# A chain of attention, MLP and routed experts on one core: the early table from six chunks of nine, for four groups

## The chip, the core and the metric

The kernel runs on one core of a Trainium2 chip. The metric is the device time of one execution in microseconds (us). Three runs of the kernel before have a median of 1148.74 us (1147.65 to 1150.2). The traced execution, from which every duration below comes, took 1151.18 us by the same clock; its span from the first to the last instruction is 1149.2 us.

## The reference, cut to what matters

```python
attn_out = _attn_ref(q, k, v)          # 4 batches, 8 heads, 576 positions, window 128
x = attn_out as 2304 tokens x 512
h = x @ w_in                           # 512 -> 2048
x = softplus(h) @ w_out                # 2048 -> 512: the tokens of the routed part
noisy = x @ w_gate + softplus(x @ w_noise) * noise
top2, top2_w = two best of 8 experts of each token, softmax over the two
for e in range(8):                     # each token goes through two experts
    out[its tokens] += weight * (relu(x[its tokens] @ w1[e]) @ w2[e])
```

## The kernel before, in words

The 2304 tokens are worked in nine **chunks** of 256 (numbers 0 to 8). The first MLP has 16 weight tiles of each of its two matrices. All chunks run its first six tiles, with the attention of the next chunk fed in between; then, one chunk after another, the other ten. A **job** is one tile of one chunk: 12 matmuls into `h`, the softplus on ACT, DVE and POOL (`mm1`, lines 564 to 574), and three jobs later 6 matmuls into `y` (`mm2`).

After its last job a chunk is routed in small steps between the jobs that follow (`route`): transposes, logits, the two best experts, and in `r_rank` each token's place in its expert's list. Four indirect DMAs per chunk from POOL (line 771) scatter the token numbers and weights into four copies of the lists in DRAM (`rect`). `mcum` holds the count of each expert so far.

The experts work on **groups**: a pair of 128 tokens of one expert (256 together), or a single 128 at the end of a list. `early_table` and `late_table` compute on DVE, in one partition, which expert and which place in its list each group has. The early table takes experts that already have 256 tokens when some chunks are still missing; the late table takes the rest. For each group `g_rows` (lines 1025 to 1039) reads the place into a register of SP, issues four small loads of the lists (`rk`, line 1032) on SP's queue, and chains a `merge` of the four copies (two short DVE reductions into `rc`, lines 1036 and 1037). `g_gather` then fetches the 256 tokens with two indirect DMAs on POOL (`xg`, line 1047); PE transposes them (`t<-ident,xg`) while the group ahead is computed, and ACT and DVE split them into `xh` and `xl` (lines 1065 and 1066).

A group has eight weight tiles of 512 KB, loaded by SP at line 1111 once the group's table is done (`raw2`, named raw in the rows, for four of them, else `rawp` in the ring of 24 slots that the first MLP's weights also use). `w2_split` makes `whi` on ACT (line 1140) and `wlo` on DVE (line 1138) from each. A pair of groups' outputs is scaled into `ys` and added into `out` by two indirect DMAs on POOL per group (line 1252); each waits for the DMA of the one before it.

Nothing is scheduled at run time. A planner (`Order`) keeps a clock of its own while the program is written out; a `chain` puts each step on its engine's queue when the planner thinks its turn has come, and the queues then run in that order. Two facts of it matter here. The SP work of `g_rows` costs nothing on the planner's clock, and a `merge` is queued a fixed time, `after=6.0`, after its loads are issued, whatever they take. A weight tile's `whi` is queued when the planner's clock has run 512 KB at 280 GB/s and 2 us more.

The main loop counts jobs with `t`. `last_start` is the first job of chunk 8's second part. `open_p2` (which frees the attention's memory and opens the pool of the tables) runs at `last_start`, and `early_table(NCH - 3)`, the table of chunks 0 to 6, one job later.

Of the kernel before, what the change touches and what calls it, by code (L numbers as in the profile page):

```python
# [25 lines left out]
class Order:  # L26
# [11 lines left out]
    def chain(self, *steps, after=0.0):  # L38

        heapq.heappush(self.heap, (self.now + after, self.count, steps, 0))  # L40
        self.count += 1
# [28 lines left out]
    def emitted(self, key):  # L70
        while key not in self.fin:
            assert self.heap, key
            self._pop()

    def need(self, key):
        self.emitted(key)
        self.now = max(self.now, self.fin[key])
# [35 lines left out]
def moe_chain_kernel(ctx, tc, qk, v, w_in, w_out, w_gate, w_noise, noise, w1, w2, out):  # L113
# [3 lines left out]
    T = B * S  # L117
    DM = H * D
    KC = DM // P
    NF = w_in.shape[0]  # L120
    E, NW1 = w1.shape[:2]
    NF1 = 2 * NW1
    CT = 256
    TT = CT // P
    NCH = T // CT
# [5 lines left out]
    NA = 6  # L131
    NCV = 5
    NPAIR = (2 * T // P + E - 1) // 2 - 3
    NSING = E - 1
    NEARLY = 5
    NOPT = 2
    NLATE = NPAIR - NEARLY
    TPAD = T + P
# [5 lines left out]
    chain, spend, need, emitted, mark = o_.chain, o_.spend, o_.need, o_.emitted, o_.mark  # L144
# [13 lines left out]
    def f32(ap):  # L158
        return ap.bitcast(F32)
# [3 lines left out]
    def tl(pool, shape, dtype, name, bufs, fin, tag=None, slots=None):  # L163

        r = rings.setdefault(name, [])
        while len(r) >= bufs:
            last = r[-bufs]
            (need if pool is psum else emitted)(last)
            if r[-bufs] == last:
                break  # L170
        r.append(fin)
        return pool.tile(shape, dtype, name=name, tag=tag or name, bufs=slots or bufs)
# [3 lines left out]
    def few_t():  # L176

        for k_ in rings["t"][-4:]:
            emitted(k_)
        nt[0] = 2  # L180
# [64 lines left out]
    x1buf = dram.tile([TPAD, DM], F32, name="x1buf")  # L245
# [13 lines left out]
    def prepare1():  # L259
        n = NREC // P  # L260
        pad = mid.tile([P, n, 2], I32, name="pad", bufs=1)
        POOL.iota(pad[:, :, 0], pattern=[[1, n]], base=0, channel_multiplier=n)
        DVE.tensor_scalar(pad[:, :, 0], pad[:, :, 0], P - 1, T, op0=OP.bitwise_and, op1=OP.bitwise_or)
        POOL.memset(f32(pad[:, :, 1]), 0.0)
        for r in rect:
            SP.dma_start(r.rearrange("(p n) z -> p (n z)", p=P), pad.rearrange("p n z -> p (n z)"))
# [193 lines left out]
    def attn_until(c):  # L460
        return 4 * attn_last(c) + 3 + LC + 1
# [148 lines left out]
    def x_load(c):  # L610
        XT[c] = tuple(tl(mid, [P, KC, CT], F32R, n, 2, ("mm1b", c)) for n in ("xh", "xl"))
        for z, x in enumerate(XT[c]):
            dma(lambda z=z, x=x: SP.dma_start(f32(x).rearrange("p k t -> p (k t)"), xspill[c, z]),
                ("xi", c, z), 1 << 19)
# [221 lines left out]
    def row(name, shape, dtype=F32):  # L836
        return p2.tile([1] + shape, dtype, name="c_" + name, tag="c_" + name, bufs=1)

    def open_p2():
        nonlocal p2  # L840
        for m in range(NM):
            emitted(("c", m))
        astack.close()
        p2 = ctx.enter_context(tc.tile_pool(name="p2", bufs=2))
        few_t()
        for name, n, base, step in (("jm", NJ, 0, P), ("jpair", NJ // 2, P, 2 * P), ("jfull", NJ // 2, 2 * P, 2 * P),
                                    ("e8", E, 0, 1), ("qe", NEARLY, 0, 1), ("qp", NLATE, 0, 1), ("qs", NSING, 0, 1)):
            t = TB[name] = row(name, [n])
            POOL.iota(t, pattern=[[step, n]], base=base, channel_multiplier=0, allow_small_or_imprecise_dtypes=True)
# [76 lines left out]
    def counted(c, name):  # L926

        need(("mc", c))
        pc = ps_t(("pc", c))[:, :E]
        mm(pc, ones, mcum, True, True)  # L930
        tb = Table(name)
        cnt = tb.row("cnt", [E])
        tb.tensor_copy(cnt, pc[0:1, :])
        tb.steps[-1] += (("pc", c),)
        return tb, cnt

    def early_table(c):
        tb, cnt = counted(c, "E")
        per = tb.above("per", cnt, TB["jfull"], NJ // 2, OP.is_ge)
        inc = tb.upto("inc", per)  # L940
        ex, r = tb.first_of(TB["qe"], "q", NEARLY, inc, per)
        tb.finish("early", ex, r, None, NEARLY)
        a, b = tb.row("a", [E]), tb.row("b", [E])
        tb.tensor_sub(b, inc, per)
        tb.tensor_scalar(a, inc, float(NEARLY), None, op0=OP.min)
        tb.tensor_scalar(b, b, float(NEARLY), None, op0=OP.min)
        tb.tensor_sub(a, a, b)
        off = TB["off"] = tb.row("off", [E])
        tb.tensor_scalar(off, a, 2.0 * P, None, op0=OP.mult)
        chain(*tb.steps, (None, 0.0, early_lists, ("tab", 0), (("scat", c),)))  # L950
# [73 lines left out]
    def g_rows(g):  # L1024

        n, eo, i = groups[g]
        eo = TB[eo]
        r0 = SP.value_load(eo[0:1, 1, i:i + 1], min_val=0, max_val=E * T)
        rc = tl(p2, [P, 2, 2], I32, "rc", 6, ("gdone", g))
        rk = tl(p2, [P, NCOPY, 2, 2], I32, "rk", 6, ("rows", g))  # L1030
        for k in range(NCOPY):
            SP.dma_start(rk[:, k, :n, :], rect[k][bass.ds(r0, n * P), :].rearrange("(a p) z -> p a z", p=P))  # L1032

        def merge():

            DVE.tensor_reduce(rc[:, :n, 0], rk[:, :, :n, 0].rearrange("p k a -> p a k"), axis=AX.X, op=OP.min)
            DVE.tensor_reduce(f32(rc[:, :n, 1]), f32(rk[:, :, :n, 1]).rearrange("p k a -> p a k"), axis=AX.X, op=OP.add)
        chain(("V", 0.4, merge, ("rows", g)), after=6.0)
        GR[g] = dict(rc=rc)

    def g_gather(g):
        n, eo, i = groups[g]
        d = GR[g]
        d["xg"] = []
        for a in range(n):
            x = tl(p2, [P, DM], F32, "xg", 6, ("gx", g, a))
            POOL.indirect_dma_start(out=x, out_offset=None,
                                    in_=x1buf[:T - 2 * CT if g < NEARLY else TPAD, :],
                                    in_offset=bass.IndirectOffsetOnAxis(ap=d["rc"][:, a, 0:1], axis=0))
            d["xg"].append(x)  # L1050

# [233 lines left out]
    def pieces_of(c):  # L1285
        for s in range(attn_until(c), attn_until(c + 1)):
            yield from attn_step(s)
# [4 lines left out]
    last_start = NT - (NF - NA)  # L1292
# [38 lines left out]
    for t in range(NT + max(L2, len(items) + 2)):  # L1331
        if t == 4:
            SP.dma_start(wgn[:, :, :E], w_gate.rearrange("(c p) e -> p c e", p=P))
            SP.dma_start(wgn[:, :, E:2 * E], w_noise.rearrange("(c p) e -> p c e", p=P))
            SP.dma_start(nz, noise.rearrange("(a p) e -> p a e", p=P))
        if t == 20:
            prepare1()
        if t > 40 and t % 2:
            p = next(zfeed, None)
            if p is not None:  # L1340
                p()
        due[0] = min(NSL, 2 * NA + max(0, t - 2 * NA + 2) // 2)
        if t in starts:
            c, n = starts[t]
            if feed is not None:
                for p in feed:
                    p()
            feed = pieces_of(c) if c + 1 < NCH else None
            total = 2 * (attn_until(c + 1) - attn_until(c)) if feed else 0
            fed, gap, gaps = 0, 0, 2 * n - 2  # L1350
        if t == last_start:
            open_p2()
        if t == last_start + 1:
            early_table(NCH - 3)
        if t < NT:
            c, fc = jobs[t]
            if c == NCH - 1 and fc == 1:
                x_load(0)
            mm1(c * NF + fc)
            if c == 0 and fc == NA + 3:  # L1360
                part_load(0)
            used(2 * fc, c)
            if NT - 3 < t:
                if t == NT - 2:
                    need(("gl", 0))
                g_transpose(0, t - NT + 2)
                if t == NT - 1:
                    turned.add(0)
                    if 3 in REG:
                        g_start(3)  # L1370
        else:
            phase2(t - NT)
        side_work()
        if 0 <= t - L2 < NT:
            c, fc = jobs[t - L2]
            mm2(c * NF + fc)
            used(2 * fc + 1, c)
            if fc == NA - 1:
                part_evac(c)
            if fc == NF - 1:  # L1380
                y_evac(c)
                rfeed = chained(rfeed, route(c))
        if 0 <= t - NT - 2 < len(items):
            s3(*items[t - NT - 2])
        side_work()
# [64 lines left out]
```

## Time and profile before

| | |
|---|---|
| median of three runs | 1148.74 us |
| traced execution | 1151.18 us, span 1149.2 us |
| mean granted clock of TensorE | 0.973 |
| PE busy | 1075.3 us (94%) |
| DVE, ACT, POOL busy | 751.0, 616.7, 518.2 us (65%, 54%, 45%) |
| chain that ended last | PE 79%, DVE 10%, DMA 3%, ACT 3%, issue 2%, SP's queue 2%, POOL 1% |

In the span's picture in 40 slices PE has 8 tenths or more in every slice from the third on but the 22nd (about 603 to 632 us) and the last one: the 22nd is at 4, and the granted clock there is at 7. That is where the last chunk of the first MLP goes over into the experts.

### The profile page before, as it was taken

Reading aid. Unit: us, or ns where it says so; the run is one execution under the profiler, and the core shown is the slowest. Engines: PE = TensorE matmul, PEld = TensorE weight load, DVE = VectorE, ACT = ScalarE, POOL = GpSimd, SP = SyncE. Lnnn points to the kernel's source line nnn. Section 1 sums busy time; section 2 is a strip of 40 time slices with the busy share of each in tenths; the row PEclk is TensorE's granted clock in tenths of the full one; section 3 lists DMA queues with packets and bytes.
Section 4 is the critical chain, followed back from the end, with each engine's and each line's share of the span. In section 5 each row is a group of like instructions: output and inputs, shape, how many; then the busy total and the mean of one; then the engine's idle time right before and its main releaser. Section 6 shows DMA issues by size and latency. Waiting matters only on the chain.

```text
span 1149.2 us, 20936 instructions
## 1 busy us (share of the span) xinstructions
PE 1075.3 (94%) x7021; PEld 916.9 (80%) x7021; DVE 751.0 (65%) x1946; ACT 616.7 (54%) x1459; POOL 518.2 (45%) x535
## 2 busy tenths in 40 slices
PE   5589998999999999999994999999999999999997
PEld 3377776777789888888873889999799799799984
DVE  7975698999785677777764678665355355355520
ACT  7776678877664444444433445555455455455531
POOL 3455577776675566666654341323223223233212
PEclk8789999999999999999997999999999999999999
DMA  8231444564583322211217976988888888888722
GB/s 302 101 92 56 161 152 164 173 227 154 187 316 120 120 74 74 74 53 60 75 20 287 333 158 160 301 213 231 266 225 226 267 233 229 267 234 233 213 58 37
DMA packets 96557, 198.91 MB, mean 173 GB/s; under 512 B 34048, under 2 KB 44800, under 8 KB 96448
## 3 DMA queue, kind: packets, MB, share of 16 engines
q1 hardware_dynamic: 86112, 176.01, 47.1%
q0 software_dynamic: 10336, 21.54, 9.0%
q8 instruction: 56, 0.92, 0.4%
q14 instruction: 53, 0.43, 0.1%
HBM read 157.82 MB, written 39.69 MB: 172 GB/s over the span
## 4 chain that ended last, share of the span: by engine, by line
PE 79%; DVE 10%; DMA 3%; ACT 3%; issue 2%; SPq 2%; POOL 1%; POOLq 0%; DVEq 0%; ACTq 0%
PE h L190 36%; PE y L190 23%; PE z L190 11%; PE t L201 4%; PE t L190 3%; PE t L339 2%; DMA raw<-in_moe_w_out 1%; ACT s L356 1%; DVE gl L572 1%; DVE s L350 1%; DVE cva L495 1%; DVE cva L496 1%; DVE cva L494 1%; SPq L1032 1%; DVE w L504 1%
## 5 line engine op out<-in xcount | busy, mean ns | idle before, releaser
L190 PE MATMUL h<-xh,w 128*128 128x256 f32 x1152 | 242.5, 293 | 14.8 <-DVE sl L568 14.7
L1252 POOL DMA_INDIRECT out<-ys,rc x41 | 82.0, 2000 | 316.6 <-DVE ys L1261 140.8
L190 PEld LDWEIGHTS h<-xh,w 128*128 128x128 f32 x1152 | 193.7, 196 | 29.2 <-DVE sl L568 20.0
L1138 DVE TENSOR_TENSOR wlo<-rawp,whi 128x1024 fp32r<-128x1024 f32 x108 | 132.0, 1222 | 126.8 <-ACT whi L1140 126.5
L1140 ACT ACTIVATE whi<-rawp 128x1024 fp32r<-128x1024 f32 x108 | 114.5, 1060 | 132.9 <-PE h L190 100.2
L190 PE MATMUL y<-w,gh 128*128 128x512 f32 x552 | 179.2, 406 | 1.1 <-DVE gh L571 1.1
L574 POOL TENSOR_TENSOR su<-sa,su 128x256 f32<-128x256 f32 x144 | 112.8, 783 | 126.0 <-DVE su L573 94.7
L190 PE MATMUL h<-xl,w 128*128 128x256 f32 x576 | 165.9, 288 | 3.6 <-DVE xl L434 3.6
L190 PE MATMUL h<-xh,whi 128*128 128x256 f32 x576 | 165.3, 287 | 0.0
L190 PE MATMUL h<-xl,whi 128*128 128x256 f32 x576 | 163.3, 284 | 0.0
L190 PE MATMUL h<-xh,wlo 128*128 128x256 f32 x576 | 163.3, 283 | 0.0
L565 ACT ACTIVATE sa<-h 128x256 f32<-128x256 f32 x144 | 54.9, 381 | 157.0 <-PE h L190 123.1
L190 PEld LDWEIGHTS h<-xl,w 128*128 128x128 f32 x576 | 112.9, 196 | 7.0 <-DVE xl L434 4.0
L569 POOL TENSOR_TENSOR sl<-sl,su 128x256 f32<-128x256 f32 x144 | 110.3, 766 | 17.8 <-DVE sl L568 6.6
L190 PEld LDWEIGHTS h<-xh,whi 128*128 128x128 f32 x576 | 110.2, 191 | 7.3 <-issue 0.7
L190 PEld LDWEIGHTS h<-xl,whi 128*128 128x128 f32 x576 | 110.3, 191 | 7.1 <-issue 1.4
L190 PEld LDWEIGHTS h<-xh,wlo 128*128 128x128 f32 x576 | 110.2, 191 | 0.0
L190 PEld LDWEIGHTS y<-w,gh 128*128 128x128 f32 x552 | 95.0, 191 | 17.9 <-issue 2.9
L190 PE MATMUL y<-w,gl 128*128 128x512 f32 x276 | 108.6, 394 | 0.6 <-DVE gl L572 0.6
L370 POOL TENSOR_TENSOR s<-s,st 128x512 f32<-128x512 f32 (+2 forms) x72 | 72.3, 1011 | 34.5 <-DVE st L362 19.9
L572 DVE TENSOR_TENSOR gl<-sl,gh 128x256 fp32r<-128x256 f32 x144 | 81.1, 564 | 9.9 <-ACT gh L570 6.8
L356 ACT ACTIVATE s<-s,st 128x256 f32<-128x256 f32 (+2 forms) x160 | 76.1, 478 | 19.7 <-DVE st L350 19.5
(258 smaller groups left out, 2255.9 us busy)
## 6 DMA issues: line engine op xcount, KB each, us to landing
rawp<-in_moe_w SPq DMA_DIRECT2D x138, 512.0 KB, 4.9
raw<-in_moe_w SPq DMA_DIRECT2D x46, 512.0 KB, 4.5
qkT<-in_qk SPq DMA_DIRECT2D x20, 512.0 KB, 5.2
raw<-in_moe_w_in SPq DMA_DIRECT2D x16, 512.0 KB, 5.9
raw<-in_moe_w_out SPq DMA_DIRECT2D x16, 512.0 KB, 6.8
out<-zero SPq DMA_DIRECT2D x19, 256.0 KB, 5.4
xspill<-xh SPq DMA_DIRECT2D x9, 512.0 KB, 2.6
xspill<-xl SPq DMA_DIRECT2D x9, 512.0 KB, 3.9
```

Of the source, the lines that this page charges most:

```text
L190: PE.matmul(o, l, r, start=start, stop=stop)
L201: PE.transpose(o, i, idn)
L339: PE.matmul(ps[j][:nq, x, :n].rearrange("p (s t) -> p s t", t=P), qkT[hd, u % NQK, 0, hp, :nq], qkT[hd, sl, 1, hp, :], start=True, stop=True)
L356: ACT.activation(s[:nq, j, :n], s[:nq, j, :n], AF.Exp, bias=st[:nq, 0, y], scale=-1.0, accum_out=st[:nq, 1, y])
L370: POOL.tensor_tensor(s[:nq, :, :n], s[:nq, :, :n], st[:nq, 3, 2 * x:2 * x + 2, None].to_broadcast([nq, 2, n]), OP.mult)
L565: chain(("A", ca(CT), lambda: ACT.activation(a, ph, AF.Abs)), ("A", ca(CT), lambda: ACT.activation(a, a, AF.Exp, scale=-1.0), ("e", t)), ( ...
L569: ("P", cg(CT), lambda: POOL.tensor_add(l, l, u), None, (("d", t),)),
L572: ("V", cv(CT), lambda: DVE.tensor_sub(gl, l, f32(gh)), ("g", t)))
L574: ("P", cg(CT), lambda: POOL.tensor_tensor(u, a, u, OP.subtract), ("d", t)), after=2 * ca(CT) + 0.15)
L1138: DVE.tensor_sub(lo, t, f32(hi))
L1140: chain(("A", ca(1024), lambda: ACT.activation(hi, t, AF.Copy), None, (("r2", j),)), ("V", cv(1024), low, ("w2", j)))
L1252: POOL.indirect_dma_start(out=out[:, :], out_offset=bass.IndirectOffsetOnAxis(ap=rc[:, a, 0:1], axis=0), in_=ys, in_offset=None, compute_o ...
```

## The change

The early table is made from the lists of chunks 0 to 5 and for four groups, in place of chunks 0 to 6 and five groups. `open_p2` runs ten jobs earlier and the table nine jobs earlier, both in chunk 7's second part. The gathers of the early groups read only the tokens of chunks 0 to 5. The late table has 14 pairs in place of 13. The call `few_t`, which brings PSUM's `t` buffers down to two, stays at `last_start`. Merges are queued 15 us (early groups) or 9 us (late groups) after their loads on the planner's clock, in place of 6 us.

```diff
-    NEARLY = 5
+    NEARLY = 4
...
         astack.close()
         p2 = ctx.enter_context(tc.tile_pool(name="p2", bufs=2))
-        few_t()
...
-        chain(("V", 0.4, merge, ("rows", g)), after=6.0)
+        chain(("V", 0.4, merge, ("rows", g)), after=15.0 if g < NEARLY else 9.0)
...
-                                    in_=x1buf[:T - 2 * CT if g < NEARLY else TPAD, :],
+                                    in_=x1buf[:T - 3 * CT if g < NEARLY else TPAD, :],
...
+        if t == last_start - (NF - NA):
+            open_p2()
+        if t == last_start - (NF - NA) + 2:
+            early_table(NCH - 4)
         if t == last_start:
-            open_p2()
-        if t == last_start + 1:
-            early_table(NCH - 3)
+            few_t()
```

From line 845 to the main loop the changed kernel's line numbers are lower by one: its 1139 is line 1140 of the kernel before.

**ACT, the first weight tile of the experts.** The place is ACT's queue in the second part of chunk 7, while chunk 6 is routed (`lgp` is a step of that). The `sa` and `sl` rows are a job's softplus; `whi<-raw` splits a weight tile of group 0.

```order
 L672 ACTIVATE lgp<-t 96x256
 L565 ACTIVATE sa<-h 128x256
-L566 ACTIVATE sa<-sa 128x256
-L567 ACTIVATE sl<-sa 128x256
+L1139 ACTIVATE whi<-raw_7510 128x1024
+L566 ACTIVATE sa<-sa 128x256
+L567 ACTIVATE sl<-sa 128x256
+L1139 ACTIVATE whi<-raw_7512 128x1024
 L565 ACTIVATE sa<-h 128x256
 L734 ACTIVATE r_a<-lg 128x16
```

Before, the first two of these splits stood ten jobs further on, in chunk 8, at the same place inside a job: between its first and its second softplus step. On SP's queue the loads of these tiles stand behind the list loads, before and now; four groups' lists are 16 loads, five groups' were 20.

**POOL, the gather of the first group of the late table.** The place is POOL's queue among the first groups of the experts. `out<-ys,rc` are the output additions (two for each pair), `rect` the scatter of chunk 8's lists, `xg<-x1buf,rc` the gathers of tokens. Before:

```order
L1252 DMA out<-ys,rc 2432x512 x2
L771 DMA rect_115<-rec,pi 18688x2
L771 DMA rect_116<-rec,pi 18688x2
L771 DMA rect_117<-rec,pi 18688x2
L1047 DMA xg<-x1buf,rc 128x512 x2
L771 DMA rect_118<-rec,pi 18688x2
L1252 DMA out<-ys,rc 2432x512 x4
L1047 DMA xg<-x1buf,rc 128x512 x4
```

Now:

```order
L1251 DMA out<-ys,rc 2432x512 x2
L771 DMA rect_115<-rec,pi 18688x2
L771 DMA rect_116<-rec,pi 18688x2
L771 DMA rect_117<-rec,pi 18688x2
L771 DMA rect_118<-rec,pi 18688x2
L1251 DMA out<-ys,rc 2432x512 x4
L1046 DMA xg<-x1buf,rc 128x512 x5
```

The gather of group 4 stood in the scatter of chunk 8; now that group 4 belongs to the late table, its two gathers stand behind the four output additions of groups 1 and 2, where those of group 5 stood and still stand.

**DVE, the merges of the late groups.** The place is DVE's queue during group 3. `gl<-h,gh` is a step of group 3, `c_Lsingleseo` the last result of the late table, `rc<-rk` a merge, `xl<-t,xh` the split of group 4's transposed tokens. Before:

```order
1576 L1191 SCALAR_TENSOR_TENSOR gl<-h,gh 128x256
1577 L1066 TENSOR_TENSOR xl<-t,xh 128x4x128
1578 L871 CAST c_Lsingleseo<-c_LBr 1x7
1579 L1138 TENSOR_TENSOR wlo<-rawp,whi 128x1024
1580 L1191 SCALAR_TENSOR_TENSOR gl<-h,gh 128x256
1581 L871 CAST c_Lsingleseo<-c_LBex 1x7
```

Now:

```order
1580 L1190 SCALAR_TENSOR_TENSOR gl<-h,gh 128x256
1581 L870 CAST c_Lsingleseo<-c_LBr 1x7
1582 L870 CAST c_Lsingleseo<-c_LBex 1x7
1583 L1035 TENSOR_REDUCE rc<-rk 128x2
1584 L1036 TENSOR_REDUCE rc<-rk 128x2
1585 L1035 TENSOR_REDUCE rc<-rk 128x2
1586 L1036 TENSOR_REDUCE rc<-rk 128x2
1587 L1065 TENSOR_TENSOR xl<-t,xh 128x4x128
```

The merges of groups 4 and 5 now stand directly ahead of the split of group 4's own tokens. Before, the first merges of late groups came ten rows further on, and were for groups 5 and 6. On PE's queue the transposes of group 4's tokens stand where they stood: behind the fourth set of 12 `h` matmuls of group 3.

## Rows read from the trace of the kernel before

**Rows 1.** Table by stages: us, length, busy of PE PEld DVE ACT POOL, clock, DMA.
```profile
600.00:620.00 20.00, 6.52 (x38) 5.31 (x37) 5.11 (x17) 6.13 (x11) 3.14 (x3) 0.67 0.54 169
```

**Rows 2.** Timeline of PE: start us, us, instruction, xcount [idle before <-releaser].
```profile
549.50 0.18 PE L190 MATMUL t<-r_mb,tri 128*128 128x8 bf16 x1
...
580.21 0.18 PE L190 MATMUL t<-r_mb,tri 128*128 128x8 bf16 x1
...
583.08 0.19 PE L190 MATMUL t<-mcum,ones 128*128 128x8 bf16 x1 [2.60 <-DVE mcum L757]
...
617.44 0.58 PE L190 MATMUL h<-xh,w 128*128 128x256 f32 x1 [13.48 <-DVE sl L568]
...
625.05 0.73 PE L190 MATMUL y<-w,gh 128*128 128x512 f32 x2 [1.14 <-DVE gh L571]
...
637.34 0.18 PE L190 MATMUL t<-r_mb,tri 128*128 128x8 bf16 x1 [1.65 <-DVE r_mb L704]
```

**Rows 3.** Timeline of ACT: a job's first softplus step, and the first tile's split.
```profile
567.59 0.39 ACT L565 ACTIVATE sa<-h 128x256 f32<-128x256 f32 x1 [1.31 <-PE h L190]
...
598.67 0.39 ACT L565 ACTIVATE sa<-h 128x256 f32<-128x256 f32 x1 [0.90 <-PE h L190]
...
613.81 1.06 ACT L1140 ACTIVATE whi<-raw 128x1024 fp32r<-128x1024 f32 x1 [14.75 <-DMA raw<-in_moe_w]
```

**Rows 4.** Timeline of SP's queue: list loads, then weight tiles.
```profile
594.81 14.55 SPq L1032 DMA_DIRECT2D rk<-rect  x20
610.17 1.93 SPq L1111 DMA_DIRECT2D raw<-in_moe_w  x4
```

**Rows 5.** Chain of waits, in order of time: the register load of the fifth list.
```profile
606.56 0.27 SPq L1028
```

**Rows 6.** Timeline of DVE: counts, softplus steps, and the early table's first result.
```profile
554.00 0.15 DVE L757 TENSOR_TENSOR mcum<-mcum,r_mb 128x8 bf16<-128x8 bf16 x1
...
558.93 0.41 DVE L568 SCALAR_TENSOR_TENSOR sl<-h,sl 128x256 f32<-128x256 f32 x1
...
587.51 0.40 DVE L568 SCALAR_TENSOR_TENSOR sl<-h,sl 128x256 f32<-128x256 f32 x1
...
589.17 0.16 DVE L871 CAST c_Eearlyeo<-c_Eqr 1x5 int32<-1x5 f32 x1
```

**Rows 7.** Table by stages behind two waits of PE: columns as in the first group.
```profile
583.10:587.00 3.90, 3.90 (x18) 3.67 (x19) 1.57 (x8) 0.80 (x2) 2.98 (x4) 0.59 0.02 1
...
617.40:622.00 4.60, 4.56 (x22) 4.30 (x23) 4.60 (x6) 3.53 (x6) 3.99 (x3) 0.67 1.02 403
```

**Rows 8.** Chain of waits: one job of PE, its h and its y matmuls.
```profile
571.90 1.44 PE h L190 x12
573.34 1.39 PE y L190 x6
```

**Rows 9.** Timeline of PE: first transposes of group 4's, then of group 5's tokens.
```profile
722.56 0.60 PE L201 MATMUL t<-ident,xg 128*128 128x128 f32 x4
...
746.00 0.60 PE L201 MATMUL t<-ident,xg 128*128 128x128 f32 x4
```

**Rows 10.** Timeline of POOL: output additions of groups 1 and 2, group 5's first gather.
```profile
696.98 2.60 POOL L1252 DMA_INDIRECT out<-ys,rc  x1 [8.41 <-ACT gh L1190]
704.66 1.59 POOL L1252 DMA_INDIRECT out<-ys,rc  x1 [5.08 <-DVE c_LBex L871]
719.30 1.57 POOL L1252 DMA_INDIRECT out<-ys,rc  x1 [13.05 <-ACT ys L1258]
725.28 2.15 POOL L1252 DMA_INDIRECT out<-ys,rc  x1 [4.41 <-DVE c_Lsingleseo L871]
734.29 1.01 POOL L1047 DMA_INDIRECT xg<-x1buf,rc  x1 [6.86 <-issue]
```

**Rows 11.** Timeline of DVE: the first merge for group 5.
```profile
733.34 0.16 DVE L1036 TENSOR_REDUCE rc<-rk 128x2 int32<-128x8 int32 x1
```

**Rows 12.** The gathers' line, 640 us to the end: from issue to landing (35 gathers).
```profile
DMA to landing us min/median/max: 4.2/6.1/7.7
```

## The prediction

> **What bounds the kernel now.** Read the picture in 40 slices first: PE is busy nearly all the span but for one dip, so time can be won or lost only where PE stands idle or slow. The table by stages puts the dip at 600 to 620 us: PE busy 6.52 of 20 us, clock 0.67 [rows 1]. The timeline of PE then names the waits around it [rows 2]: 2.60 us for the count that opens the early table, 13.48 us for a softplus step of DVE, 1.14 us for another and 1.65 us in chunk 7's ranking. What all that costs is read from the rankings, which come once per chunk: chunk 5's at 549.50, chunk 6's at 580.21, chunk 7's at 637.34 [rows 2]. The undisturbed period is 30.71 us, the disturbed one 57.13. The second holds eight transposes more (0.60 us a set of four, overlapping their neighbours [rows 9]; I count 1.0). So the change of phase loses 57.13 - 30.71 - 1.0 = 25.4 us.
>
> The largest part has one cause. ACT ended a job's first step at 598.67 + 0.39 and then waited 14.75 us for the first weight tile of the experts, with the job's other steps behind it [rows 3]. SP issued that tile's load only at 610.17, because 20 list loads took 14.55 us on its queue [rows 4]; the tile landed 613.81 - 610.17 = 3.64 us later. ACT's 14.75 us became 13.48 us of PE. The slow clock comes on top: behind the 2.60 us wait it was at 0.59 for 3.90 us, behind the long one at 0.67 for 4.60 us [rows 7], that is 1.6 and 1.5 us.
>
> **The change, part by part.**
>
> *The count.* It moves nine jobs forward in order, to one job behind chunk 5's ranking: 549.50, some 0.15 for the ranking's five matmuls, one job of 1.44 + 1.39 [rows 8], so PE is there at 552.5. The count is complete at 554.00 + 0.15 [rows 6]. PE waits 1.6 us where it waited 2.60, and I leave the slow clock at 1.6: 3.2 us. The table's 20 short DVE steps and the index patterns on POOL lie beside PE's work, as they did; were DVE late with them, about 1 us of PE, which is in the range.
>
> *The first weight tile.* SP's order inside this piece is unchanged: list loads, then tiles; only four lists in place of five. ACT's row for the first split also stands at the same place in a job, now in the job whose first step ran at 567.59 [rows 3]. So the wait is moved, not removed. The table's first result stands in DVE's order behind the softplus step of 558.93; before, it came 589.17 - 587.51 = 1.66 us after such a step, with fewer rows between [rows 6], and I take 2. With PE's 3.2 us of delay it is ready at 558.93 + 2 + 3.2 = 564.1. A register load and the first issue are about 1.4 (an estimate: the fifth list's register load began at 606.56 [rows 5] and its loads ended at 609.36, four issues and this step in 2.8 us; the first one is longer): 565.5. Four lists take 606.56 - 594.81 = 11.75 [rows 4, 5], the step to the first tile 610.17 - 609.36 = 0.8, landing 3.64: 581.7. ACT is there at 567.59 + 0.39 + 3.2 = 571.2 and waits 10.5 us; less the 1.3 us that PE's buffers covered before, 9.2 us of PE, and 1.5 for the clock: 10.7.
>
> *The rest of that phase.* What of the 25.4 us is in none of these is 25.4 - 2.60 - 1.6 - 13.48 - 1.5 = 6.2: the waits of 1.14 and 1.65 and a second dip of the clock, all left by DVE and POOL catching up with ten splits, ten merge steps and four gathers at once. Now the splits and gathers are spread over chunk 8 in all three queues and the lists are there long before their merges. But the two splits and four merges fall into chunk 6's own ranking steps. I keep 3.0 of the 6.2, between nothing and all of it.
>
> So 3.2 + 10.7 + 3.0 = 16.9 us stand against 25.4: a gain of 8.5. Bounds: 12.5 (the table 1 us earlier, nothing left to catch up) and 4.
>
> *Group 4, the new member of the late table.* The late table cannot come earlier; it needs chunk 8. Before, its first group was 5; now it is 4, wanted one group of 23.4 us sooner (746.00 - 722.56 [rows 9]). PE's queue has the transposes of group 4's tokens where they were, 722.56 on the old clock. POOL's queue now has the gather behind both output additions of group 2, which ran at 719.30 and 725.28 to 727.43 [rows 10]; these follow PE's work on group 2 and shift with it. So relative to PE nothing moves: the gather issues at 727.7, and 35 gathers took 4.2, 6.1 and 7.7 us (least, median, most) to land [rows 12]. PE stands from 722.56 to 733.8, 11.2 us, and the slow clock costs 1.5 (as behind the 13.48 us): a loss of 12.7. The merge ahead of it on DVE also follows PE's fourth step of group 3, but ends before POOL is free, so it adds nothing. Behind the waiting PE the split of these tokens holds up DVE, whose next weight tiles are needed only later. Bounds: fastest landing, 9.3 + 1.5 = 10.8; slowest landing, with the two additions as far apart as group 1's, 704.66 - 696.98 = 7.68 in place of 5.98 [rows 10], 14.5 + 1.5 = 16.0. Group 5's gather follows at once and has 23 us; before, it was merged at 733.34 [rows 11], issued at 734.29 and landed by the median at 740.4, 5.6 us ahead of its use.
>
> The DMA landing time is where a page speaks otherwise. The Trainium skill (DMA: Bandwidth & Descriptors, section Anatomy of one DMA, SWDGE path) fits 2.0 us plus the bytes at 436 GB/s for a DMA from GpSimd; for 256 KB that is 2.6 us, an estimate from that page. By it the loss would be 5.1 + 2.6 + 1.5 = 9.2 and the sum 0.7 slower. The trace's fastest gather took 4.2, so the row decides here.
>
> *Elsewhere:* the number of pairs and singles is the same (4 + 14 pairs for 5 + 13), so PE's work is; the 32 early weight tiles are loaded in chunk 8, beside matmuls, and those of group 4 wait for the late table but have more than a group's time.
>
> **The sum** is 12.7 - 8.5 = 4.2 us slower. The traced execution took 1151.18 us (span 1149.2), 2.4 above the median of the runs; from the median, 1148.74 + 4.2 = 1152.9.
>
> **Rivals.**
> 1. *Group 4's tokens are there in time.* Then only the gain is left: 1148.74 - 8.5 = 1140.2. For it: the late table's pairs were known on DVE long before group 5's merge, and no gather made PE wait in the old trace. Against: two queues in fixed order. It decides at the issue: the gather would have to go out 6.1 us before 722.56, at 716.5, ahead of group 2's first addition. Chance 0.11.
> 2. *The tile wait vanishes*, because ACT comes later or the lists go faster than I read: 10.7 us less, 1142.2. It would need the tile 9 us sooner, the table's first result at 555, about when its count is only taken. Chance 0.09.
> 3. *A second gather of the late table is also late*, for instance the single behind group 5: another 12.7, 1165.6. Against: their merges stand well ahead of their transposes. Chance 0.06.
> 4. *The gather lands as fast as SP's tile did*, in 3.64 us for twice the bytes [rows 3, 4]: idle 5.1 + 3.64 = 8.8, loss 10.3, sum 1.8 slower, 1150.5, which no measurement tells from no change. Against: no gather of the trace was under 4.2. Chance 0.05. The Trainium skill's fit above (DMA: Bandwidth & Descriptors) points the same way, at 0.7 slower.
> 5. *Gain and loss cancel otherwise, or the moved table changes nothing:* 1148.7. The orders show that the change is real. Chance 0.03.
>
> **How the numbers follow.** My forecast has 0.66, its own range is from 12.5 gained and 10.8 lost (1147.0) to 4 gained and 16.0 lost (1160.7). A measurement of this kernel can tell 0.2%, 2.3 us, from no change. Of the 0.66 about 0.53 lie above 1151.0 and 0.12 between, 0.01 below; with rival 3 slower is 0.59, with rivals 4 and 5 same is 0.20, with rivals 1 and 2 faster is 0.21. The range for 8 in 10 leaves out rival 1, rival 3 and little else: 1142 to 1160.5.
>
> **What would show it.** Right: in the timeline of PE a wait of about 1.6 us near 552, one of 8 to 11 us near 575 with ACT waiting for raw, none above 3 us where chunk 8 ends, and one of 9 to 14 us ahead of group 4's transposes, some 8 us earlier on the clock than 722, with POOL's gather issued after group 2's second addition. Wrong: no wait at group 4 (rival 1), ACT's first split without a wait (rival 2), or a further wait behind group 5 (rival 3).

## The result, and the profile after

The changed kernel took 1153.89 us (median of five runs, 1153.34 to 1157.72) against 1148.74 us (five runs, 1146.42 to 1150.78): a ratio of 1.0054, 95% interval 1.003 to 1.0078. It is slower by 3.4 to 9.0 us; 1152.9 was forecast. Its traced execution has a span of 1151.5 us.

The timeline of PE after, columns as in [rows 2]: the rankings of chunks 5, 6 and 7, the three waits between them, and the transposes of group 4's and group 5's tokens.

```profile
544.85 0.18 PE L190 MATMUL t<-r_mb,tri 128*128 128x8 bf16 x1
...
549.55 0.18 PE L190 MATMUL t<-mcum,ones 128*128 128x8 bf16 x1 [1.50 <-DVE mcum L757]
...
577.80 0.58 PE L190 MATMUL h<-xh,w 128*128 128x256 f32 x1 [8.45 <-DVE sl L568]
...
592.22 0.18 PE L190 MATMUL t<-r_mb,tri 128*128 128x8 bf16 x1 [3.18 <-DVE r_mb L704]
...
625.48 0.18 PE L190 MATMUL t<-r_mb,tri 128*128 128x8 bf16 x1
...
723.94 1.08 PE L201 MATMUL t<-ident,xg 128*128 128x128 f32 x4 [14.63 <-DMA xg<-x1buf,rc]
...
748.70 0.60 PE L201 MATMUL t<-ident,xg 128*128 128x128 f32 x4
```

From chunk 5's ranking to chunk 7's are 625.48 - 544.85 = 80.63 us, where [rows 2] has 87.84: 7.2 us won. From there to group 4's transposes are 98.46 us, where [rows 2, 9] have 85.22: 13.2 us lost. That is the one wait of 14.63 us less some 1.5 us that the clock gave back: behind the count of the late table it was slow in the kernel before and full here (last section), which is luck and no part of the change. Group 5 follows 24.76 us behind group 4 instead of 23.44 [rows 9], 1.3 us lost to the slow clock behind that wait. One more thing must be taken out of the comparison: chunk 5's ranking itself is 4.65 us earlier than in [rows 2], though hardly anything ahead of it was changed. The eleven profiles of this study have it anywhere from 544.85 to 549.65, so two traces are best compared from this ranking on: 1151.5 - 544.85 = 606.65 against 599.70, 6.95 us longer, or some 8.5 without the clock's 1.5.

ACT's timeline after, the first split of a weight tile and the softplus step ahead of it (before: [rows 3]):

```profile
565.04 0.39 ACT L565 ACTIVATE sa<-h 128x256 f32<-128x256 f32 x1 [1.31 <-PE h L190]
574.90 1.06 ACT L1139 ACTIVATE whi<-raw 128x1024 fp32r<-128x1024 f32 x1 [9.47 <-DMA raw<-in_moe_w]
```

SP's queue after, list loads and first tiles (before: [rows 4]), then the loads around group 4's wait:

```profile
559.21 11.32 SPq L1031 DMA_DIRECT2D rk<-rect  x16
571.34 1.94 SPq L1110 DMA_DIRECT2D raw<-in_moe_w  x4
...
702.38 2.34 SPq L1031 DMA_DIRECT2D rk<-rect  x4
704.95 5.88 SPq L1110 DMA_DIRECT2D rawp<-in_moe_w  x8
```

POOL's timeline after: the two output additions of group 2 and group 4's first gather (before: [rows 10]).

```profile
705.89 1.55 POOL L1251 DMA_INDIRECT out<-ys,rc  x1 [16.37 <-ACT ys L1257]
715.34 1.55 POOL L1251 DMA_INDIRECT out<-ys,rc  x1 [7.90 <-DMA out<-ys,rc]
717.20 1.01 POOL L1046 DMA_INDIRECT xg<-x1buf,rc  x1 [0.30 <-issue]
```

The first of these additions in the chain that ended last, from its start until it had landed:

```profile
705.89 8.70 DMA out<-ys,rc
```

In the kernel before, the landing of group 2's first addition, and that of all additions from 660 to 1140 us (least, median, most):

```profile
DMA to landing us min/median/max: 5.2/5.2/5.2
...
DMA to landing us min/median/max: 4.7/6.7/9.3
```

DVE's timeline after: the last result of the late table and the merge for group 4 right behind it (before: [rows 11]).

```profile
710.17 0.15 DVE L870 CAST c_Lsingleseo<-c_LBex 1x7 int32<-1x7 f32 x1
710.25 0.14 DVE L1035 TENSOR_REDUCE rc<-rk 128x2 int32<-128x8 int32 x1
```

The table by stages after, columns as in [rows 1]: behind the waits of 1.50, 8.45 and 3.18 us, behind the count of the late table, and behind the wait of 14.63.

```profile
549.50:553.50 4.00, 3.95 (x28) 3.70 (x29) 3.40 (x13) 1.22 (x3) 3.33 (x4) 1.00 0.05 5
577.80:583.00 5.20, 5.20 (x18) 4.71 (x19) 4.75 (x13) 2.42 (x9) 4.51 (x6) 0.50 0.94 352
594.00:598.00 4.00, 4.00 (x19) 3.42 (x18) 1.81 (x4) 2.05 (x4) 2.72 (x3) 0.62 0.01 1
662.60:666.00 3.40, 3.39 (x21) 3.07 (x22) 3.19 (x9) 1.22 (x2) 1.03 (x1) 1.00 0.26 49
723.90:727.00 3.10, 3.06 (x10) 2.67 (x11) 0.69 (x1) 0.60 (x1) 0.00 (x0) 0.54 0.22 87
```

PE's pattern is the one forecast: a short count wait at full clock, a tile wait cut from 13.48 to 8.45, none above 2 us where chunk 8 ends, and a long one at group 4.

### The profile page after: what moved, and what is told of

Its sections match the earlier page's. It is cut to its first block, busy times and chain, and to the rows that moved or that the text cites. A ratio compares the mean times of both kernels' runs of the same rounds, so it can differ in the third digit from the quotient of the medians.

```text
span 1151.5 us, 20919 instructions
## 1 busy us (share of the span) xinstructions
PE 1073.7 (93%) x7021; PEld 915.6 (80%) x7021; DVE 749.4 (65%) x1946; ACT 616.6 (54%) x1459; POOL 507.4 (44%) x535
## 4 chain that ended last, share of the span: by engine, by line
PE 77%; DVE 11%; DMA 4%; ACT 4%; issue 2%; SPq 1%; POOL 1%; POOLq 0%; ACTq 0%
PE h L190 35%; PE y L190 23%; PE z L190 10%; PE t L201 4%; PE t L190 3%; PE t L339 2%; DMA raw<-in_moe_w_out 1%; DVE s L350 1%; ACT s L356 1%; DVE w L504 1%; DMA out<-ys,rc 1%; DVE cva L495 1%; DVE cva L496 1%; DVE cva L494 1%; DVE gl L572 1%
## 5 line engine op out<-in xcount | busy, mean ns | idle before, releaser
L190 PE MATMUL h<-xh,w 128*128 128x256 f32 x1152 | 239.5, 291 | 9.5 <-DVE sl L568 9.4
L190 PEld LDWEIGHTS h<-xh,w 128*128 128x128 f32 x1152 | 191.5, 193 | 23.5 <-DVE sl L568 14.5
L1137 DVE TENSOR_TENSOR wlo<-rawp,whi 128x1024 fp32r<-128x1024 f32 x105 | 128.3, 1222 | 119.4 <-ACT whi L1139 119.3
L1139 ACT ACTIVATE whi<-rawp 128x1024 fp32r<-128x1024 f32 x105 | 111.3, 1060 | 119.0 <-PE h L190 88.9
L573 DVE TENSOR_SCALAR su<-sa 128x256 f32<-128x256 f32 x144 | 61.7, 428 | 38.6 <-ACT sa L566 37.9
```

The source lines that it names most:

```text
L190: PE.matmul(o, l, r, start=start, stop=stop)
L573: chain(("V", cv2(CT), lambda: DVE.tensor_scalar(u, a, 1.0, 1.0, op0=OP.add, op1=OP.subtract), None, (("e", t),)), ("P", cg(CT), lambda: P ...
L1137: DVE.tensor_sub(lo, t, f32(hi))
L1139: chain(("A", ca(1024), lambda: ACT.activation(hi, t, AF.Copy), None, (("r2", j),)), ("V", cv(1024), low, ("w2", j)))
```

## The experiments

My theory: two waits in two stages decide the time, each made by the order of queues (SP's list loads ahead of the first tile; POOL's additions, and DVE's late table, ahead of group 4's gather). The main rivals: the DMA engines are the limit at group 4; the phase is bound by how late the table comes; the merges' place matters by itself. All runs in one table: PE's anchors from the profiles, in us, and the medians with the ratio to the kernel before, run beside each (medians 1148.6 to 1148.7).

| kernel | chunk 5 ranked at | to chunk 7's ranking | to group 4's transposes | to the end | median | ratio, 95% interval |
|---|---|---|---|---|---|---|
| before | 549.50 | 87.84 | 85.22 | 426.64 | 1148.7 | 1 |
| changed | 544.85 | 80.63 | 98.46 | 427.56 | 1153.9 | 1.0054 (1.003 to 1.0078) |
| pairs first | 547.36 | 80.55 | 84.31 | 426.28 | 1140.5 | 0.9935 (0.9913 to 0.9957) |
| tiles first | 546.79 | 67.67 | 100.68 | 427.86 | 1145.9 | 0.9985 (0.9971 to 0.9999) |
| both | 546.06 | 69.14 | 84.42 | 426.38 | 1128.9 | 0.9837 (0.9822 to 0.9853) |
| before, tiles first | 546.48 | 89.44 | 83.70 | 426.48 | 1149.1 | 1.0012 (0.9999 to 1.0025) |
| before, four groups | 548.34 | 87.09 | 100.77 | 428.00 | 1165.0 | 1.0142 (1.0117 to 1.0167) |
| merges at 6 | 548.75 | 79.97 | 100.33 | 428.35 | 1158.3 | 1.0084 (1.0069 to 1.01) |
| before, lists split | 546.51 | 75.21 | 85.14 | 426.64 | 1135.5 | 0.9883 (0.9864 to 0.9903) |
| both, splits later | 548.73 | 73.02 | 86.71 | 426.24 | 1132.4 | 0.986 (0.9843 to 0.9877) |
| gather between | 549.65 | 79.74 | 95.43 | 428.48 | 1154.3 | 1.0044 (1.0027 to 1.0061) |

**Pairs first.** In the late table, group 4 is released between the pairs and the singles, and with it its list loads, its merge, its gathers and its weight tiles:

```diff
+        tb.steps.append((None, 0.0, None, ("tab", 1), (("scat", c),)))
+        tb.steps.append((None, 0.0, pump))
         gq = tb.row("gq", [NSING])
...
-        chain(*tb.steps, (None, 0.0, None, ("tab", 1), (("scat", c),)), (None, 0.0, pump))
+        chain(*tb.steps, (None, 0.0, None, ("tab", 2)), (None, 0.0, pump))
...
-        if g >= sure[0] or ("tab", int(g >= NEARLY)) not in o_.fin:
+        if g >= sure[0] or ("tab", int(g >= NEARLY) + (g > NEARLY)) not in o_.fin:
```

> The changed kernel, with one edit: the late table's pairs are released before its singles are computed, for group 4 alone, so that its list is merged on DVE some 40 rows earlier and its two gathers stand on POOL's queue ahead of group 2's two output additions instead of behind them. My theory (the gather is late because of its place in two queues; PE's 14.63 us ahead of group 4's transposes are all due to it): gather issued by 700, landed by 706, no wait of PE over 2 us ahead of group 4's transposes (about 709), and 14.63 + 1.3 us of slow clock behind it less: 1153.9 - 15.9 = 1138.0, between 1136 and 1141. Rival (something else makes PE wait there, such as group 4's weight tiles, which compete with the gathers for the DMA engines): a wait of 5 us or more stays at that place, 1144 or more.

1140.5 us, as the theory has it. POOL's timeline and PE's in this kernel: the first gather goes out ahead of the additions, and the transposes wait for nothing.

```profile
698.05 1.31 POOL L1048 DMA_INDIRECT xg<-x1buf,rc  x1 [5.18 <-issue]
708.96 1.62 POOL L1253 DMA_INDIRECT out<-ys,rc  x1 [8.32 <-ACT ys L1259]
```

```profile
712.22 0.60 PE L201 MATMUL t<-ident,xg 128*128 128x128 f32 x4
```

The way to group 4 is 98.46 - 84.31 = 14.15 us shorter, and 1.28 us less come behind it. The loss is one wait of the gather, and the earlier place of group 4 in the queues removes it.

**Tiles first.** SP loads four weight tiles ahead of the lists:

```diff
-        chain(*tb.steps, (None, 0.0, early_lists, ("tab", 0), (("scat", c),)))
+        chain(*tb.steps, (None, 0.0, None, ("tab", 0), (("scat", c),)), (None, 0.0, tiles_lists))
...
+    def tiles_lists():
+        for _ in range(NXTRA):
+            w2_load()
+        early_lists()
```

> The changed kernel, with one edit: SP issues the first four weight tiles ahead of the 16 list loads instead of behind them. My theory (ACT's wait for the first tile is SP's queue): first tile issued near 560 and landed near 564, no wait of ACT over 2 us at its first split, no wait of PE over 2 us there, the lists 2 us later without harm because their merges stand 12 us later in DVE's queue; 8.45 us of PE and 2.6 us of clock less: 1153.9 - 11.05 = 1142.9, between 1140 and 1146. Rival A (the lists are late next: a wait at their merges takes the place of the one removed): 1150 or more. Rival B (the clock was the larger part, and stays slow for other reasons): 1146 to 1150.

1145.9 us, at the upper end of the range. ACT's first split and PE's ranking of chunk 6 in this kernel:

```profile
565.57 1.05 ACT L1139 ACTIVATE whi<-raw 128x1024 fp32r<-128x1024 f32 x1
```

```profile
582.65 0.18 PE L190 MATMUL t<-r_mb,tri 128*128 128x8 bf16 x1 [2.89 <-DVE r_mb L704]
```

```profile
582.60:588.00 5.40, 5.35 (x39) 4.97 (x40) 3.42 (x17) 2.65 (x6) 2.98 (x2) 1.00 0.18 69
```

ACT waits for no tile; the phase is 12.96 us shorter, more than the 11.05 expected. The wait at chunk 6's ranking stays, but the clock behind it is at 1.00 here, as the table by stages above shows, where it was at 0.62 in the changed kernel: 1.5 us of the difference. The way to group 4 is 2.2 us longer, of which 1.5 is a slow clock behind the late table's count (last section).

**Both edits.**

> The changed kernel with both edits of the first two experiments: group 4's pair released ahead of the singles, and the first four weight tiles issued ahead of the list loads. My theory (two separate waits in two stages, so the gains add): the first edit alone measured 1140.5, 13.4 under the changed kernel, the second alone 1145.9, 8.0 under it; together 1153.9 - 13.4 - 8.0 = 1132.5, between 1129 and 1135; no wait of PE above 4 us between chunk 5's ranking and the last group. Rival (the stages share a limit, such as the weight stream of SP: what is won in chunk 8 is waited for later): 1138 or more.

1128.9 us, 1.6% under the kernel before and 25.0 us under the changed one, where the two edits alone sum to 21.4: a hair below my range. From chunk 5's ranking on the traces add up better, 26.7 us against 15.5 + 10.4. PE reaches chunk 6's ranking with the wait of 2.89 us left, and group 4's transposes with none:

```profile
581.91 0.18 PE L190 MATMUL t<-r_mb,tri 128*128 128x8 bf16 x1 [2.89 <-DVE r_mb L704]
...
699.62 0.60 PE L201 MATMUL t<-ident,xg 128*128 128x128 f32 x4
```

No shared limit shows, and this version beats both kernels.

**The kernel before, tiles first, merges later** (`after=15.0 if g < NEARLY else 9.0` in place of `after=6.0`).

> The kernel before, with two edits: SP issues the first four weight tiles ahead of the 20 list loads, and the merges of the lists are queued later, as in the change (15 and 9 in place of 6); the early table stays where it was. If the tile wait were all that costs there (rival), its 13.48 us of PE and 1.5 us of clock would go: 1148.7 - 15.0 = 1133.7. My theory: with the table this late, the last of the five lists lands near 614 whatever stands ahead of it, and the five merges stand together in DVE's queue near 606 to 608, ahead of softplus steps and of the first transposes; so a wait of some 5 to 10 us at the merges or at group 0's tokens takes the place of the one removed: 1141, between 1137 and 1147.

1149.1 us, nothing won: a miss, above my range. A wait did take the place of the one removed, but it is 20 us where I said 5 to 10. SP's queue, ACT and PE in this kernel:

```profile
591.58 1.94 SPq L1111 DMA_DIRECT2D raw<-in_moe_w  x4
594.39 15.42 SPq L1032 DMA_DIRECT2D rk<-rect  x20
610.00 0.34 SPq L1111 DMA_DIRECT2D rawp<-in_moe_w  x1
```

```profile
613.77 1.06 ACT L1140 ACTIVATE whi<-rawp 128x1024 fp32r<-128x1024 f32 x1 [9.72 <-DMA rawp<-in_moe_w]
```

```profile
625.39 1.09 PE L201 MATMUL t<-ident,xg 128*128 128x128 f32 x4 [20.15 <-DMA xg<-x1buf,rc]
```

I had overlooked the fifth tile: its load is behind the 20 lists now, ACT waits 9.72 us for it, DVE's merges stand behind that split, and PE waits 20.15 us for group 0's tokens. The phase is 1.6 us longer than before.

**The kernel before with four early groups** (`NEARLY = 4`, nothing else).

> The kernel before, with one edit: four early groups in place of five, the table where it was. It takes the change's loss alone. My theory: group 4's gathers stand behind group 2's output additions as in the change, PE waits 11 to 15 us ahead of their transposes plus 1.3 us of clock (12.3 to 16.3; I take 14); the list loads are 16 for 20, 2.8 us off the wait for the first tile: 1148.7 + 14 - 2.8 = 1159.9, between 1157 and 1163. Rival (the wait at group 4 comes from the phase having become shorter, so that POOL or DVE is behind only in the changed kernel): 1146 to 1149, without a wait at group 4.

1165.0 us, 16.3 slower and above my range: I had 14 for group 4, less 2.8 for the lists. PE in this kernel:

```profile
613.54 0.58 PE L190 MATMUL h<-xh,w 128*128 128x256 f32 x1 [10.62 <-DVE sl L568]
...
623.13 0.88 PE L201 MATMUL t<-ident,xg 128*128 128x128 f32 x4 [3.54 <-DMA xg<-x1buf,rc]
...
736.20 1.09 PE L201 MATMUL t<-ident,xg 128*128 128x128 f32 x4 [16.93 <-DMA xg<-x1buf,rc]
```

The tile wait shrank by 2.86 us as expected, but group 0's tokens, covered by it before, now cost 3.54, and group 4's wait is 16.93. So the loss belongs to having four groups in the early table; the gain, which is missing here, belongs to the rest of the change, above all the table's earlier place.

**The changed kernel with merges queued at 6.**

> The changed kernel with its second part undone: merges of lists queued with 6 everywhere, as before, in place of 15 and 9. My theory (with list loads ahead of the tiles on SP's queue, the lists have landed when the first tile's split ends, so the eight merge steps of 0.16 us may stand anywhere behind it; and the late groups' merges stay behind the singles of the late table): the same time, 1153.9, between 1151.5 and 1156. Rival (the later merges are what keeps DVE free for chunk 6's ranking): 2 us or more slower, with a longer wait than 3.2 us of PE ahead of that ranking.

1158.3 us, above my range; its interval overlaps the changed kernel's. But the trace does not put it at the merges: the phase is 79.97 us, 0.7 shorter, and the wait at chunk 6's ranking is 2.72 in place of 3.18.

```profile
595.45 0.18 PE L190 MATMUL t<-r_mb,tri 128*128 128x8 bf16 x1 [2.72 <-DVE r_mb L704]
```

From chunk 5's ranking on, this trace is 2.0 us longer, 1.5 of it again the clock behind the late count; the other 3.9 us of its longer span lie ahead of that ranking, where the programs are the same. So the rival's place is refuted. Whether the later merges are worth a few us elsewhere stays open.

**The kernel before, lists split.** The table and its five groups as before; SP loads group 0's list, five tiles, then the other lists, and the merges of these lists stand later on DVE:

```diff
-        chain(*tb.steps, (None, 0.0, early_lists, ("tab", 0), (("scat", c),)))
+        chain(*tb.steps, (None, 0.0, None, ("tab", 0), (("scat", c),)), (None, 0.0, tiles_lists))
...
-        chain(("V", 0.4, merge, ("rows", g)), after=6.0)
+        chain(("V", 0.4, merge, ("rows", g)), after=6.0 if g == 0 else 24.0 if g < NEARLY else 6.0)
...
+    def tiles_lists():
+        g_rows(0)
+        while w2_load():
+            pass
+        chain((None, 3.0, None), (None, 0.0, lambda: [g_rows(g) for g in range(1, NEARLY)]))
```

> The kernel before, its early table and its five early groups where they were; only SP's order and the merges' places differ: group 0's list first, then the first five weight tiles, then the lists of groups 1 to 4, and the merges of groups 1 to 4 some 40 rows later on DVE. My theory (what made PE wait in chunk 8 was the order of one queue, not how late the table came; the experiment with four tiles ahead of all lists failed since it left the fifth tile and group 0's list behind 20 and 12 loads): first tile landed near 600, group 0's gathers issued near 602, no wait of PE above 5 us in chunk 8; of 13.48 + 1.5 + some 3 of catching up, 12 to 17 are won: 1134.5, between 1131 and 1140. Rival (at this place the table is too late for five groups, whatever the order): a wait of 8 us or more at group 0's or group 1's tokens, 1143 or more.

1135.5 us, as the theory has it: 13 us won with the table left where it was. SP's queue and PE:

```profile
591.92 2.18 SPq L1032 DMA_DIRECT2D rk<-rect  x4
594.91 2.69 SPq L1111 DMA_DIRECT2D raw<-in_moe_w  x4
597.78 0.33 SPq L1111 DMA_DIRECT2D rawp<-in_moe_w  x1
598.91 12.62 SPq L1032 DMA_DIRECT2D rk<-rect  x16
```

```profile
602.43 0.39 PE L190 MATMUL h<-xh,w 128*128 128x256 f32 x1 [1.34 <-DVE sl L568]
...
607.38 0.63 PE L201 MATMUL t<-ident,xg 128*128 128x128 f32 x4
```

The wait of 13.48 us came from what stood in front of what, on SP's queue and on DVE's, not from the table's lateness. How much each of the two queues gave is not told apart.

**Both edits, splits later.** In the version with both edits the first two splits are queued 16 us later, the merges at 17 in place of 15:

```diff
-        chain(("DMA", (1 << 19) / 280e3, None), (None, 2.0, None, ("r2" if n == 2 else "w2", j)))
+        chain(("DMA", (1 << 19) / 280e3, None), (None, 18.0 if j < 2 else 2.0, None, ("r2" if n == 2 else "w2", j)))
```

> The version with both edits (1128.9), with the first two splits of weight tiles moved on DVE from before chunk 6's ranking to behind its r_mb step, and the eight merge steps with them. My theory (the 2.89 us that PE still waits ahead of chunk 6's ranking is DVE's time for two splits of 1.2 us and the merges, 8 x 0.08 us apart, in front of r_mb): the wait falls under 0.8 us, 2.2 to 2.9 us and up to 1 us of clock less: 1126.0, between 1124 and 1128. Rival (the ranking is late of itself, by the early table's 20 steps ahead of it on DVE or by the softmax steps): the wait stays above 2 us and the time within 1 us of 1128.9.

1132.4 us, 3.5 slower than both edits alone and above my range: a miss in the sum. The wait did go, so its cause is shown, the splits and merges together; other waits took its place. The traced execution took 1136.8 us, the slowest of the four.

```profile
581.52 0.18 PE L190 MATMUL t<-r_mb,tri 128*128 128x8 bf16 x1
...
589.28 0.39 PE L190 MATMUL h<-xh,w 128*128 128x256 f32 x1 [1.73 <-DVE sl L568]
...
604.26 0.73 PE L190 MATMUL y<-w,gh 128*128 128x512 f32 x2 [1.50 <-DVE gh L571]
...
621.75 0.18 PE L190 MATMUL t<-r_mb,tri 128*128 128x8 bf16 x1 [1.70 <-DVE r_mb L704]
```

Chunk 5's to chunk 6's ranking took 32.79 us in place of 35.85, and chunk 6's to chunk 7's 40.23 in place of 33.29. I read this as DVE time that some job must carry; no run shows it by itself.

**Gather between.** In the changed kernel, group 2's second addition is queued behind the gathers:

```diff
-                chain(ev, ("P", 1.1, put, ("yo", g, a)))
+                chain(ev, (None, 14.0 if g == 2 and a == 1 else 0.0, None), ("P", 1.1, put, ("yo", g, a)))
```

> The changed kernel, with one edit: group 2's second output addition is queued later, so that group 4's and group 5's gathers stand between group 2's two additions on POOL instead of behind both. My theory (of the 14.63 us the larger part is the second addition, which waits for the first one's landing: 7.90 us in the changed kernel's profile; I had taken the two as far apart as before, 5.98 us): the gather goes out right behind the merge, at about 710.5 on the changed kernel's clock, lands 6 us later, and PE waits 7 us in place of 14.63: 1153.9 - 7.6 = 1146.3, between 1144 and 1149. Rival (the DMA engines are the limit there, and the gather lands late whenever it is sent): a wait of 11 us or more, 1150 or more.

1154.3 us, above my range: no gain that the runs can tell. POOL, PE, and DVE's merge for group 4 in this kernel:

```profile
712.13 1.55 POOL L1251 DMA_INDIRECT out<-ys,rc  x1 [15.27 <-DVE ys L1260]
717.42 1.01 POOL L1046 DMA_INDIRECT xg<-x1buf,rc  x1 [3.73 <-issue]
```

```profile
724.82 1.09 PE L201 MATMUL t<-ident,xg 128*128 128x128 f32 x4 [9.27 <-DMA xg<-x1buf,rc]
```

```profile
716.48 0.14 DVE L1035 TENSOR_REDUCE rc<-rk 128x2 int32<-128x8 int32 x1
```

PE's wait is 9.27 us, neither 7 nor 11. Group 4 was due at 724.82 - 9.27 = 715.55; the gather left 1.9 us after that, where it left 7.9 after it in the changed kernel, so the second addition had held it up by 6.0 us. What holds it now is the merge, which starts 0.9 us after group 4 was due, behind the singles of the late table on DVE; and then 7.4 us pass until PE has the tokens, against 6.7 there. From chunk 5's ranking on the trace is 3.0 us shorter than the changed kernel's, after 1.5 us lost to the clock behind the late count; the medians do not show even that.

## Why the prediction was right, point by point

**The count.** PE waited 1.50 us where 1.6 was said. The 1.6 us of slow clock did not come: the clock stayed at 1.00 behind the wait. So this term is 1.7 us too large.

**The first weight tile.** The chain held link by link, to within 1.6 us. Counted from chunk 5's ranking, the first list load was forecast 16.0 us later and came after 14.4; the lists took 11.3 us (11.75), the step to the tile 0.8 (0.8), the landing 3.56 (3.64). ACT waited 9.47 (10.5) and PE 8.45 (9.2). Behind it PE ran 5.20 us at 0.50, the lower level of the clock, which costs 2.6 us, not 1.5. Together 11.05 for 10.7.

**The rest of the phase.** I kept 3.0 of 6.2 us because two splits and four merges fall into chunk 6's ranking steps. That place was right: 3.18 us, of which the merges make 0.5 (2.72 us with the merges elsewhere); with the splits and merges moved behind it, the wait was gone. But the wait brings 4.00 us at 0.62 behind it, 1.5 us more. In all the phase lost 80.63 - 2 x 30.71 - 1.0 = 18.2 us, forecast 16.9; the gain is 7.2, forecast 8.5. That the two are so near is partly luck: the count was 1.7 us too dear, the rest too cheap by more.

**Group 4** is the term that was mis-sized. The wait came where it was said and by the mechanism that was said, with 14.63 us in place of 11.2, just past the end of its range (14.5). The step that failed is "so relative to PE nothing moves". Group 4 was due at 723.94 - 14.63 = 709.31. The first addition went out 3.4 us ahead of that, as before (3.3). The second came 9.45 us behind the first, where I took 5.98 from [rows 10]: it waits for the first one's landing, which took 8.70 us in this trace and 5.2 before. The trace of the kernel before already had landings up to 9.3 us; I sized the gap by one pair of additions and bounded it by one other. Nor is it a chance of one trace. The two additions of group 2 stand 8.91 to 10.03 us apart in all four kernels that have them ahead of group 4's gather (changed, tiles first, before with four groups, merges at 6), and 5.98 to 6.46 apart in the six that have five early groups or release group 4 ahead of the singles. While the first addition was under way SP sent group 4's eight weight tiles in 5.88 us, and in the other three of the four as many in 6.03 to 7.33; in "pairs first" they were out 12 us ahead of it. That these tiles slow the addition is likely, but no run changes them alone. So the gather left 7.9 us late, not 5.1, and was there at most 6.74 us later (6.1). The clock took 1.3 (1.5). Together 15.9 us, forecast 12.7.

By the Trainium skill's fit (DMA: Bandwidth & Descriptors, Anatomy of one DMA, SWDGE path) such a gather takes 2.6 us, an estimate from that page. The trace does not agree: of the gathers whose landing it tells, none took under 3.5. ([rows 12], too, is of such gathers alone, 30 of its 35.)

**The sum.** 7.2 won, 13.2 + 1.3 lost, 0.4 won later: 6.95 us from chunk 5's ranking on, where 4.2 was forecast; 5.15 by the medians. Both terms missed to the same side, by 1.3 and 3.2 us with group 4's full 15.9, and the clock behind the late count hid 1.5 of that. So the mechanism was right, but that 1152.9 came within 1.0 us of the median is luck in part: the traces alone put the cost of the change at some 8.5 us, and the first half, which the change hardly touches, scatters by 4.8.

**The rivals.** That group 4's tokens are in time (rival 1) fails at two gates, not one: even with the second addition out of the way the merge is late, and only the release ahead of the singles made it true. That the tile wait vanishes (rival 2) needs SP's order changed, as "tiles first" did. No further gather of the late table was late (rival 3). Group 4's gather did not land in 3.64 us (rival 4): 6.74 passed until PE had it.

## What to carry to other kernels

Before a table or a load is moved to an earlier stage, look at what stands in front of the late item on its own queue: here 13 us were to be had by reordering SP's loads and DVE's merges and leaving the table alone, and 25 us (20 against the kernel before) by two such edits of the changed kernel. When an item moves from an early to a late batch, follow it through every queue that it must pass (merge on DVE, gather on POOL), and release it as soon as its own inputs are there, not with the last of the batch. When a wait is taken away, list what else stands behind the same block: in the kernel before, four tiles ahead of the lists won nothing while the fifth tile stayed behind them.

## What the runs showed of the hardware

**The same wait, with and without a slow clock.** PE's wait of 1.97 to 1.98 us for the late table's count stands in all eleven profiles. Behind it the granted clock was at 1.00 in six of them and between 0.59 and 0.72 in five, the kernel before among them; the stretch between the two sets of transposes around it is 8.3 us in the former and 9.85 in the latter. The table by stages behind this wait in the kernel before (the changed kernel's is the fourth row of its table above, at 1.00):

```profile
674.40:678.00 3.60, 3.54 (x13) 3.06 (x14) 2.30 (x9) 1.06 (x1) 0.40 (x1) 0.59 0.75 181
```

So 1.5 us between two profiles of this kernel can be the clock alone. Waits of 8.45 us and more were followed by a granted clock of 0.50 to 0.67 in every profile that has one.

**What it costs that output additions wait for one another.** The program has each wait until the one before it has landed. The list of waits of the changed kernel has these over its whole length (us in total, times, longest); at group 2 the landing was 8.70 us, beside 5.2 in the kernel before:

```profile
POOL out L1251 <- DMA out<-ys,rc: 49.9, 9, 8.3
```

**The first half scatters.** Chunk 5's ranking moved over 4.8 us between profiles of the changed kernel and of its variants, which are the same up to there, about as much as the change itself is worth.
